# Rows, feature parts, masks and PSUM copies given other engines, with a new order of every queue

## The chip, the cores and the metric

One core of one Trainium2 chip. The time is device microseconds of one execution of the whole program, the median of several runs. The engines are called as the profile calls them: PE (TensorE), ACT (ScalarE), DVE (VectorE), POOL (GpSimd) and SP (SyncE, which here issues DMAs).

## What is computed

Four blocks, one after the other, on a sequence of 2048 tokens of width 512 with 32 heads of 16: attention with a compressive memory (A), a linear attention (B), then A and B once more. Each block adds its result to x.

```
def _A_ref(x, wq, wk, wv, wo, beta):            # x has been layer-normed
    ...
    for s in range(N):                          # N = 4 segments of L = 512 tokens
        qs, ks, vs = (q[:, :, s].copy(), k[:, :, s].copy(), v[:, :, s].copy())
        logits = jnp.einsum('bhqd,bhkd->bhqk', qs, ks) * scale + mask   # causal in the segment
        p = _softmax(logits, axis=-1)
        a_dot = jnp.einsum('bhqk,bhkd->bhqd', p, vs)
        pq = phi(qs)                            # phi(t) = t + 1 where t > 0, else exp(t)
        num = jnp.einsum('bhld,bhde->bhle', pq, M)
        den = jnp.einsum('bhld,bhd->bhl', pq, z)[..., None] + 1e-06
        o = g * (num / den) + (1.0 - g) * a_dot
        outs.append(o)
        pk = phi(ks)
        M = M + jnp.einsum('bhld,bhle->bhde', pk, vs)
        z = z + jnp.einsum('bhld->bhd', pk)
    ...
x = x + _A_ref(_layernorm(x, axis=-1), A_wq, A_wk, A_wv, A_wo, A_beta)
x = x + _B_ref(_layernorm(x, axis=-1), B_wqkv, B_w_phi, B_wo)
```

B projects to q, k and v, makes of q and of k the softmax features of a small product per head (and of its negative), sums feature-times-value over all tokens, and divides as usual.

## The kernel before, in words

**Tiles.** x stays in SBUF as 16 tiles of 128 tokens by 512. A layer (L is 0 or 1) is one A and one B. It is staged by segment s = 0 to 3 of four tiles:

- `ln` makes the layer norm of a segment. For each tile DVE takes the statistics (L786, L787), POOL raises the variance to the power -1/2 (L798) or ACT does it by logarithm and exponential (L792, L793), and DVE makes the normalised rows `xn` (L802, one instruction a tile with two scalars a row). A DMA on SP's queue, or PE with a copy out of PSUM, transposes them.
- `a_proj` projects to keys, queries and values. PSUM is emptied by copies (`k.copy`, `q.copy`, `v.copy`, all at L563) that either ACT or DVE can do. For the memory it makes phi as the smaller of exp(t) and max(t + 1, 1): ACT makes the exponential (L933, L958), DVE the linear part (`phik.lin` L934, `phiq.lin` L959) and the minimum (L935, L960). `lo` (L892) and `kp` (L923) are copies within SBUF.
- `a_att` is the attention inside the segment. Its scores come in units of 2048 columns of PSUM, and each unit is read by two exponentials (L1103) of 128x1024. There are 36 of them in a segment and 288 in the program. Units with a diagonal block are masked after the exponential: two products with the mask `modd` for the odd heads (`mask.odd`, L1109, DVE or POOL) and one `affine_select` in place for the even heads (`mask.even`, L1112, POOL). `mask.even` comes after both `mask.odd` of its tile, since it overwrites what they read. Then PE multiplies with the values, and DVE divides (L1137, L1138).
- `a_out` projects the result and adds it to x. `b_keys`, `b_queries` and `b_out` are the linear attention: `b_keys` adds up over the segments what `b_out` multiplies with, so `b_out` of a layer starts when `b_keys` of segment 3 is complete. The next layer's first `ln` follows `b_out` of segment 0. This passage between the 144th exponential (the last of layer 0) and the 145th (the first of layer 1) is called the boundary here; what comes after the 288th is called the tail.

**The order of the work.** Nothing is scheduled at run time. The functions above only list 3388 operations with their reads and writes. Four tables say the rest. `ORDER` names every operation once; the order of the names, taken for each engine alone, is the order of that engine's queue (a negative entry is a filler of some matmuls into an unused part of PSUM). `ENGINE` has one letter (a, d, p, s) for each operation that several engines can do, in the order in which the functions list them. `SLOTS` says which buffer a tile gets. `AFTER` is a list of pairs (x, y): operation x also waits for operation y, beyond what its data ask for. `replay` (L354) reads them, and `finalize` (L407) writes the instructions and the semaphore waits.

`either` (L559) lists an operation that DVE or POOL can do, with the time of each that was assumed; `dve`, `pool` and `act` list one for a single engine.

Of the kernel before, what the change touches and what calls it, by code (L numbers as in the profile page):

```python
# [8 lines left out]
ALU = mybir.AluOpType  # L9
AX = mybir.AxisListType  # L10
BF16 = mybir.dt.bfloat16
# [512 lines left out]
class Kernel:  # L524
# [65 lines left out]
    def sb(self, name, shape, dt):  # L590
        return self.es.enter_context(self.nc.sbuf_tensor(name, shape, dt))
# [891 lines left out]
```

## Time and profile before

| | |
|---|---|
| three runs | 442.88, 443.93, 445.04 us; median 443.93 us |
| the profiled execution | span 442.2 us from the first instruction to the last; no other time is given for it |
| granted TensorE clock | 0.996 |
| instructions with busy time | PE 7894, DVE 1032, ACT 625, POOL 446 |
| the first exponential of the attention starts | 12.82 us |
| the 144th starts; the 145th starts | 182.84 us; 221.22 us |
| the 288th ends | 397.97 us |

How to read it: an engine's busy time is the time in which at least one of its instructions runs. ACT, DVE and PE overlap the end of one instruction with the start of the next, so that the mean duration of an instruction is more than what it takes of its engine's time; lines that give the time of several equal instructions in a row show the latter. A wait is put down to the engine that ended it.

### The profile page before, as it was taken

The numbers are of one execution on the slowest core, as the hardware profiler recorded it, in microseconds if no ns is written. First come the engines' busy times: TensorE is split into PE (matmuls) and PEld (weight loads), VectorE is DVE, ScalarE is ACT, GpSimd is POOL, SyncE is SP. The second block draws the span as 40 slices with busy tenths as digits, with TensorE's granted clock in tenths as the row PEclk, the third lists the DMA queues.
The fourth block names the chain that finished last, engine by engine and source line by source line (L and its number), as shares of the span: only waits on it lengthen the run. The fifth ranks groups of instructions, "written<-read, shape, count | busy, mean of one in ns | idle before, by whom it ended". The sixth has DMA issues, their size and how long they took to land.

```text
span 442.2 us, 18441 instructions
## 1 busy us (share of the span) xinstructions
PE 423.6 (96%) x7894; PEld 295.4 (67%) x7955; DVE 414.2 (94%) x1032; ACT 406.9 (92%) x625; POOL 268.3 (61%) x446
## 2 busy tenths in 40 slices
PE   7999999999999999999999999999999999999997
PEld 6877767666756665757777666776576665575763
DVE  6999999999999998799999999999899999979997
ACT  3999999999999999997799999999999999999731
POOL 4587679656676687331364778567766767744200
PEclk9999999999999999999999999999899999999999
DMA  8999532517212521532665335444135333032396
GB/s 241 203 221 131 96 51 50 96 29 97 50 26 49 67 35 31 94 61 51 128 75 86 64 73 99 75 72 75 27 39 85 44 57 51 1 74 45 69 164 203
DMA packets 117201, 36.35 MB, mean 82 GB/s; under 512 B 108928, under 2 KB 117120, under 8 KB 117120
## 3 DMA queue, kind: packets, MB, share of 16 engines
q1 hardware_dynamic: 114432, 32.80, 43.2%
q10 hardware_dynamic: 2688, 2.37, 1.7%
q8 instruction: 63, 1.03, 1.0%
q14 instruction: 18, 0.15, 0.1%
HBM read 6.32 MB, written 2.10 MB: 19 GB/s over the span
## 4 chain that ended last, share of the span: by engine, by line
ACT 65%; PE 29%; DVE 4%; issue 1%
ACT PT L1103 49%; PE PS L504 27%; ACT Ek L1199 6%; ACT phi L958 3%; ACT phi L933 2%; ACT K L1282 2%; PE PS L1438 1%; PE PS L585 1%; ACT ktok L563 1%; DVE Vt L1227 1%; ACT VT L563 1%; ACT EQ L1282 1%; ACT QT L563 1%; DVE KV L1254 1%; DVE Rkv L1256 1%
## 5 line engine op out<-in xcount | busy, mean ns | idle before, releaser
L1103 ACT ACTIVATE PT<-PS 128x1024 bf16<-128x1024 f32 x288 | 281.8, 1112 | 1.6 <-PE PS L504 1.1
L1109 POOL TENSOR_TENSOR D<-PT,modd 128x256 bf16<-128x256 bf16 x130 | 85.8, 674 | 43.5 <-ACT PT L1103 13.2
L1112 POOL TENSOR_SCALAR_AFFINE_SELECT PT<-PT 128x512 bf16<-128x512 bf16 x128 | 80.8, 642 | 35.0 <-DVE D L1109 21.6
L504 PEld LDWEIGHTS PS<-VT,PT 128*128 128x128 bf16 x2048 | 74.1, 96 | 15.3 <-ACT PT L1103 1.6
L504 PE MATMUL PS<-VT,PT 128*128 128x17 bf16 x2048 | 79.6, 171 | 0.9 <-ACT PT L1103 0.4
L504 PE MATMUL PS<-VT,D 128*128 128x17 bf16 x512 | 59.7, 171 | 0.1
L504 PE MATMUL PS<-QT,K 32*128 32x64 bf16 (+2 forms) x2176 | 56.0, 213 | 1.6 <-ACT PT L1103 0.8
L786 DVE BATCH_NORM_STATS2 stats<-X 128x6 f32<-128x512 bf16 x64 | 43.0, 681 | 1.7 <-DMA X<-in_A_x_dram 1.4
L504 PEld LDWEIGHTS PS<-VT,D 128*128 128x128 bf16 x512 | 43.2, 96 | 0.2 <-issue 0.2
L1164 DVE TENSOR_TENSOR X<-X,PS 128x512 bf16<-128x512 bf16 x60 | 40.0, 675 | 2.9 <-PE PS L504 2.1
L504 PEld LDWEIGHTS PS<-QT,K 32*128 32x128 bf16 x2176 | 29.5, 93 | 18.7 <-ACT PT L1103 11.5
L1227 DVE TENSOR_TENSOR Vt<-PS,Zk 128x1024 bf16<-128x1024 f32 (+1 forms) x34 | 38.8, 1153 | 1.2 <-PE PS L504 0.9
L1199 ACT ACTIVATE Ek<-PS 128x512 bf16<-128x512 f32 x64 | 38.0, 682 | 1.1 <-PE PS L504 1.0
L1109 DVE TENSOR_TENSOR D<-PT,modd 128x256 bf16<-128x256 bf16 x126 | 35.0, 302 | 1.2 <-PE PS L504 0.7
L504 PE MATMUL PS<-WA_v,xA 128*128 128x256 bf16 x256 | 35.2, 273 | 0.1
L504 PE MATMUL PS<-WA_k,xA 128*128 128x256 bf16 x256 | 34.7, 275 | 0.3 <-ACT PT L1103 0.2
L504 PE MATMUL PS<-xA,WA_q 128*128 128x256 bf16 (+1 forms) x272 | 34.4, 267 | 0.1
L1302 POOL COPY O<-rho 128x512 bf16<-128x512 bf16 x29 | 16.9, 616 | 25.3 <-PE PS L504 9.1
L504 PE MATMUL PS<-WA_o,OT 128*128 128x512 bf16 x113 | 30.5, 380 | 1.7 <-issue 0.5
L1206 POOL TENSOR_TENSOR Vt<-Ek 128x512 f32<-128x512 bf16 x24 | 27.6, 1154 | 6.8 <-ACT Ek L1199 5.3
L1138 DVE TENSOR_TENSOR O<-PS,r 128x256 bf16<-128x256 f32 (+1 forms) x72 | 27.4, 385 | 1.2
L504 PEld LDWEIGHTS PS<-WA_k,xA 128*128 128x128 bf16 x256 | 23.2, 98 | 6.6 <-ACT PT L1103 1.1
(163 smaller groups left out, 921.1 us busy)
## 6 DMA issues: line engine op xcount, KB each, us to landing
X<-in_A_x_dram SPq DMA_DIRECT2D x3, 512.0 KB, 7.5
out_dram<-X ACTq DMA_DIRECT2D x10, 128.0 KB, 2.1
EQ<-in_B_wqkv_dram SPq DMA_DIRECT2D x2, 512.0 KB, 7.1
out_dram<-X SPq DMA_DIRECT2D x6, 128.0 KB, 2.4
OT<-O SPq DMA_TRANSPOSE x36, 3.2
WA_o<-in_A_wo_dram SPq DMA_DIRECT2D x1, 512.0 KB, 6.4
WB_v<-in_B_wqkv_dram SPq DMA_DIRECT2D x1, 512.0 KB, 7.1
WB_o<-in_B_wo_dram SPq DMA_DIRECT2D x1, 512.0 KB, 3.9
```

The costliest lines, as they stand in the source:

```text
L504: return e.matmul(o, l, r, start=st, stop=sp, tile_position=(basep(l), basep(o)))
L786: self.dve(lambda e, t=t, src=src: e.bn_stats(self.stats[:, t, :], src()), 0.603, [held() if held else R("X", t)], [R("stats", t)], name=" ...
L958: self.act(lambda e, t3=t3, src=src, two=two: e.activation(two(), src(), ACT.Exp), 512, [sres], [t3()], name="phiq.exp", cost=0.48)
L1103: self.act(lambda e, st=st, pt=pt: e.activation(pt.ap[:].rearrange("p b c -> p (b c)"), self.ps[:, st.slot[0] * 512:st.slot[0] * 512 + 102 ...
L1109: self.either(lambda e, d=d, k=k, pt=pt: e.tensor_tensor(d.ap[:, :, k, :].rearrange("p b (z c) -> p b z c", z=2), self.ends(pt.ap[:, :, 25 ...
L1112: self.pool(lambda e, q=quarters: e.affine_select(q(), q(), [[0, 4], [1, 128]], ALU.is_ge, 0.0, base=0, channel_multiplier=-1), 0.6, [pt() ...
L1138: self.dve(lambda e, r1=r1, view=view, nt=nt, g=g, o=o[ts]: e.tensor_tensor(o.ap[:, 0:nt, g, :].rearrange("p i (h d) -> p i h d", d=DH), v ...
L1164: self.dve(lambda e: e.tensor_tensor(X[:, t, :], X[:, t, :], self.bank(gen), ALU.add), 0.6, [R("X", t), gen()], [R("X", t)], name="resid")
L1199: self.act(lambda e, sgn=sgn, Ek=Ek, gen=gen: e.activation(Ek.ap[:, sgn, :], self.bank(gen), ACT.Exp, scale=1.0 - 2.0 * sgn), 512, [gen()] ...
L1206: self.pool(lambda e, Ek=Ek, sums=sums: e.tensor_tensor(sums(), *(Ek.ap[:].rearrange("p s (h j) -> p s h j", h=H)[:, :, :, 8 * k:8 * k + 8 ...
L1227: self.dve(lambda e, w=w, n=n, Vt=Vt, Zk=Zk, gen2=gen2: e.tensor_tensor(self.signed(Vt)[:, w, :, 0:16], self.bank(gen2).rearrange("p (h d) ...
L1302: P.add(("act", "pool"), {"act": lambda e, dst=dst, src=src: e.activation(dst(), src(), ACT.Copy), "pool": lambda e, dst=dst, src=src: e.t ...
```

## The change

Four operations get a second engine, and one constant is added for that:

- `xn` (L802) may be done by DVE or POOL.
- `phik.lin` (L934) and `phiq.lin` (L959) may be done by DVE or POOL.
- `mask.even` (L1112) may be done by POOL as before, or by DVE as a product with a triangular mask `tri` of 128x128 that POOL makes once in `setup` by two more instructions.

```
+        self.tri = sb("tri", [128, 128], BF16)
...
+        pool(lambda e: e.memset(self.tri[:], 1.0), 0.2, (), [R("tri")], name="tri")
+        pool(lambda e: e.affine_select(self.tri[:], self.tri[:], [[1, 128]], ALU.is_ge, 0.0, base=0, channel_multiplier=-1), 0.3, [R("tri")], [R("tri")], name="tri")
...
-                self.dve(lambda e, t=t, n=n, xn=xn: e.tensor_scalar(xn.ap[:, n], self.X[:, t, :], self.mv[:, t, 0:1], self.rstd[:, t:t + 1],
+                self.either(lambda e, t=t, n=n, xn=xn: e.tensor_scalar(xn.ap[:, n], self.X[:, t, :], self.mv[:, t, 0:1], self.rstd[:, t:t + 1],
...
-                    self.dve(lambda e, kt=kt, dst=dst: e.tensor_scalar(heads(dst()), self.spread(kt), 1.0, 1.0, op0=ALU.add, op1=ALU.max), 0.21, [kt()], [res], port=True, name="phik.lin")
+                    self.either(lambda e, kt=kt, dst=dst: e.tensor_scalar(heads(dst()), self.spread(kt), 1.0, 1.0, op0=ALU.add, op1=ALU.max), 0.21, 0.62, [kt()], [res], name="phik.lin")
...
-                    self.pool(lambda e, q=quarters: e.affine_select(q(), q(), [[0, 4], [1, 128]], ALU.is_ge, 0.0, base=0, channel_multiplier=-1), 0.6, [pt()], [pt("e")], name="mask.even")
+                    P.add(("dve", "pool"), {"dve": lambda e, q=quarters: e.tensor_tensor(q(), q(), self.tri[:, None, :].to_broadcast([128, 4, 128]), ALU.mult),
+                                            "pool": lambda e, q=quarters: e.affine_select(q(), q(), [[0, 4], [1, 128]], ALU.is_ge, 0.0, base=0, channel_multiplier=-1)},
+                          {"dve": 0.336, "pool": 0.6}, [pt(), R("tri")], [pt("e")], lat=0.05, port=True, name="mask.even")
```

`phiq.lin` changes as `phik.lin` does. All four tables are new. `ORDER` names 3390 operations and 6 fillers with 45 matmuls (before: 14 fillers with 67). `AFTER` has 36 pairs (before: 173). Read along the list of operations, the letters of `ENGINE` give these counts (instructions before -> after):

| operation | ACT | DVE | POOL |
|---|---|---|---|
| `xn` | | 64 -> 5 | 0 -> 59 |
| `phik.lin`, `phiq.lin` | | 46 -> 30 | 0 -> 16 |
| `mask.even` | | 0 -> 2 | 128 -> 126 |
| `mask.odd` | | 126 -> 162 | 130 -> 94 |
| `k.copy`, `q.copy`, `v.copy`, `fold.copy` (PSUM, 512 wide) | 36 -> 24 | 66 -> 78 | |
| `xnT.copy`, `boT.copy` (PSUM, after a transpose by PE) | 16 -> 9 | 4 -> 11 | |
| `kp`, `lo` | 1 -> 0 | 29 -> 20 | 34 -> 44 |
| `bk.z`, `bq.wide` | 5 -> 0 | 6 -> 1 | 53 -> 63 |

The place of an operation in `ORDER` against the four marks (first, 144th, 145th and last exponential in ACT's queue) says in which stretch it is issued. Between the first and the 144th, ACT's queue has 3 `v.copy`, one `k.copy`, one `q.copy` and one `fold.copy` fewer. In the boundary it has 4 `xnT.copy`, one `bq.wide` and one `bk.z` fewer. Between the 145th and the last it has two each of `k.copy`, `q.copy` and `v.copy`, one `lo` and one `bk.z` fewer and one small `bq.ln` more. In the tail it has 3 `boT.copy`, 2 `bq.wide` and one `bq.ln` fewer.

PE's queue has, in the boundary, 2 steps of `bk`, 3 of `bout` (two 512-wide matmuls each), one `bo` (8 matmuls), 2 steps of `kv` (4 each), 2 of `bq.sum` (16 each) and 4 of `pv` (8 each) fewer, which stand in the stretches before and after it. In the tail it has 2 steps of `bk`, 2 of `bq` and 5 of `pv` fewer.

More of the change, by code (lines that the diff above doesn't have):

```diff
@@ L33 @@
 ORDER = (
[134 rows of a table removed]
[135 rows of a table added]
 )
 AFTER = (
[17 rows of a table removed]
[4 rows of a table added]
 )
 ENGINE = (
-    "aaddpaadpaapadapaaddddpapddaddddppdpdpddddpdppppppppdppppddppdpddapaddddpaddddddaddddaddpdpdpppppdppppppddddppddddppddpppdpppdddpdddddpapdda"
-    "ddpdddpdpdddpdppppppdddddddpdpppddddddppppppddppdpppppddddpddadaddddddpdddddpppppppadppdddpdddddppdddddppdppdpddpppdddppddaadpapppppaaaaaada"
-    "papdpadaaadddddapdaaddddddddppdddpdddppdppppppddppddpdpddadadadapaddpdadapppppappppppdppdpdddddpdddpdpdppppppppdpddddapdpadadapdddaapddadppp"
-    "pppppppddddpddddddddddpppdpddpppppddppddpdddpdpdadpdddpddddddpppppppddddppddddddpdpdpddppppdppddddppddppdddappppapppasaassaaasasaaasaaaa"
+    "dadapdpdpaadpadpadapaapddpdpappdddpdpdpppppdppddpddpddpdppdppdpppdppppdppddppdpddpppppddpdddaddapdpdpdpddpdpddddddadddddddpppdppppppppddpppp"
@@ new lines @@
+    "pppddpppppdppdpddpddpdpddpddpddppdddppddpddpddpppppdpdadddpaddddpdpddddpddpdpdppppppppppppddpddpdppddpddppdpddpddpddpppdpppdpppppppddppppddp"
+    "ddpppppdpdpdddpdpdpdpdddpdddddpppppdppppppddppdpddppdpdpdddpdppddpddddpddpddpdppdddpppdpdppddpddpppdpappppppppaaaapdpdpdpdpappddadpaaapddddp"
+    "dddddaddpddppdppppdppddpdppddpddpdppppppppddpdpppdpddppppppdpddpaddadddapdppapddddpapdpppppppppppppppdpppppdppddpdppddppdpddppppppppppdpddpd"
+    "ppddpddppdpppdpapddpaddaddpdpdpddpapddddpdpppppppppppppdpddpddppdpppppdpddpdppddddpdpppdpddpppppppdppdppddppppddddpdpdddddddpdddpdddddpppdpp"
@@ L193 @@
+    "ppppppddpddpdppddpddpddpddppppddddpddppppdppddddpddppppddpddpppdpappppppppaadssaaaaasaaaasdsds"
 )
 SLOTS = (
-    "30101150011223200020110010002313101120134730120130561306072238931260120031343012032004317301151224020321063154592010111207206821031601011502"
-    "16910100178210111016201005100020321400235903114250236703320315013241060013031202612230714134920250001257235606812710630313130200121000001021"
-    "15235702104022304013013003901020001333160010001100021201110148021221131200020116920200010100184200110321201110201202040130961003201510324830"
@@ L198 @@
-    "32570101300012011010100313169130060702024831036213353010450230127012030810322412030313016270134531063082120011122101113701001320112002802145"
-    "10000002120100317302405002341602051089021014003020215012453003410233501141602050001110030203000100057202201420136451271006022110112200270110"
-    "63021145120208902145012023200101210002312136007051100021400102011220261200015102000132220371213017236121100021300203302631071011026111842010"
-    "10400521010012102105100403121200012911341220101062020105910110300021431022010110068012311460503130027901100011233101030001000241002121002030"
@@ L206 @@
-    "10011114120413167126004108912600710021211030511031002003023410200011441060014111532000040012230151202200102134702100201106123200154501303404"
-    "1513609146175129003332003351015622307"
+    "10112020011032140192010001161203150217016013322004150246327164783213007160331201210013015310612332709213617187210060011271106412706312120161"
+    "02117420015821219110212031273131200670461313001731171321270628223405300215603453422305114002113702010010901018212010365100201301243000422502"
+    "01903261175011240752010324362000013401053122011100132450254087031321133102225033364102212131335010211783031345124203101109010013320451351303"
@@ new lines @@
+    "32020236132601725130209321412403005024125115301302273100011367683111230030310032025913161121717132162053212254139300050862041501234135703593"
+    "20041142301504761000673232545002100512109220040503204120041106072038211612003502120271712001216113101214601002332210820101023131104501123101"
+    "20167102032211280132393031453005303220130713100326200104130006612012111772003130700637000221602200407611000200232013233300534050202303861013"
+    "20660402012000331200041562131138611021951221017320121010410011330121210911001085012221021371001320240031000430521130693014501230221012115200"
@@ new lines @@
+    "46022490032158313121401002130020100331126930203010120062022540102820350002430102001501118402014206702100231221951000013120627141202011100231"
+    "31110810211000259102330204523030232120142176305023020023041150013803220495201011103122061726210678732111501410230200402035230067691210602131"
+    "10761453230701312272132316708221013210710312130543110600704051623613393172301610101031212137047121126217520952314070212334362354142011000911"
+    "20115410200630201040291326732243170060121707121212602318217016242231040500570200141617016138127310122101101033120140050693020223022421002001"
@@ L208 @@
+    "30122101792010301436560201418202214424320601410601301203931330053041150072501506102321100300363013114014302211652200320240321012056770116012"
+    "1715096223270103234213032643761801704"
 )
@@ L801, in ln @@
             for n, t in enumerate(4 * c + i for i in grp):
-                self.dve(lambda e, t=t, n=n, xn=xn: e.tensor_scalar(xn.ap[:, n], self.X[:, t, :], self.mv[:, t, 0:1], self.rstd[:, t:t + 1],
-                                                                    op0=ALU.subtract, op1=ALU.mult), 0.324,
-                         [R("X", t), R("mv", t), R("rstd", t)], [xn(n)], port=True, name="xn")
+                self.either(lambda e, t=t, n=n, xn=xn: e.tensor_scalar(xn.ap[:, n], self.X[:, t, :], self.mv[:, t, 0:1], self.rstd[:, t:t + 1],
+                                                                       op0=ALU.subtract, op1=ALU.mult), 0.324, 0.65,
+                            [R("X", t), R("mv", t), R("rstd", t)], [xn(n)], name="xn")
             if len(grp) == 2:
@@ L958, in a_proj @@
                         self.act(lambda e, t3=t3, src=src, two=two: e.activation(two(), src(), ACT.Exp), 512, [sres], [t3()], name="phiq.exp", cost=0.48)
-                        self.dve(lambda e, dst=dst, src=src: e.tensor_scalar(dst(), src(), 1.0, 1.0, op0=ALU.add, op1=ALU.max), 0.21, [sres], [res], port=True, name="phiq.lin")
+                        self.either(lambda e, dst=dst, src=src: e.tensor_scalar(dst(), src(), 1.0, 1.0, op0=ALU.add, op1=ALU.max), 0.21, 0.62, [sres], [res], name="phiq.lin")
                         self.dve(lambda e, two=two, dst=dst: e.tensor_tensor(dst(), dst(), two(), ALU.min), 0.334, [res, t3()], [res], port=True, name="phiq.min")
```

4 lines of the change are left out of this document (removed), and 290 rows, old and new, of tables (AFTER, ORDER).

## The prediction

> **What bounds the kernel now.** I read the page's busy shares and slices first, then the busy times in five stretches cut at the marks of the attention (front, layer 0, boundary, layer 1, tail), then the chain that ended last, as a whole and in the two stretches without exponentials.
>
> ```profile
> span 442.2 us, 18441 instructions
> PE 423.6 (96%) x7894; PEld 295.4 (67%) x7955; DVE 414.2 (94%) x1032; ACT 406.9 (92%) x625; POOL 268.3 (61%) x446
> PE   7999999999999999999999999999999999999997
> DVE  6999999999999998799999999999899999979997
> ACT  3999999999999999997799999999999999999731
> POOL 4587679656676687331364778567766767744200
> ACT 65%; PE 29%; DVE 4%; issue 1%
> ```
>
> ```profile
> 0.00:12.82 12.82, 10.56 (x120) 8.92 (x121) 8.97 (x32) 5.79 (x11) 5.80 (x21) 1.00 0.87 256
> 12.82:183.90 171.08, 164.43 (x3466) 116.78 (x3487) 162.93 (x430) 170.96 (x225) 122.42 (x200) 1.00 0.49 82
> 183.90:221.20 37.30, 36.62 (x419) 25.05 (x421) 36.59 (x78) 29.74 (x81) 10.56 (x18) 1.00 0.37 72
> 221.20:397.97 176.77, 171.50 (x3510) 119.61 (x3536) 166.24 (x427) 175.19 (x232) 122.04 (x195) 0.99 0.40 62
> 397.97:442.20 44.23, 40.44 (x395) 25.02 (x396) 39.47 (x69) 25.25 (x81) 7.52 (x14) 0.99 0.55 120
> ...
> ```
>
> ```profile
> by line: PE PS L504 72.8%; PE PS L585 5.8%; DVE Rkv L1256 3.5%; DVE KV L1254 3.4%; DVE Vt L1227 3.3%; ACT Ek L1199 2.8%; issue 1.7%; PE PS L1438 1.6%; ACT OT L563 1.5%; DVE EQ L1308 1.5%; ACT Vt L1219 0.9%; ACT Zk L1215 0.6%; ACT Zk L1214 0
> by line: PE PS L504 55.8%; issue 4.5%; DVE Vt L1227 4.3%; DVE PT L1338 4.1%; PE PS L585 3.6%; DVE KV L1254 2.9%; DVE Rkv L1256 2.9%; DVE X L1164 2.7%; DVE PhiK L1308 2.6%; DVE Zk L1210 2.2%; DVE EQ L1308 1.3%; ACT xB L563 1.3%; ACT O L1302
> ```
>
> The columns of the second fence are the stretch, its length, then the busy time of PE, PE's weight loads, DVE, ACT and POOL. ACT is busy for 170.96 of 171.08 us in layer 0 and for 175.19 of 176.77 in layer 1: there it sets the pace, and the whole chain is ACT for 65%. PE looks nearly as full, but its digits are weak evidence, as the first row below says: a weight load waited 72 times for an exponential, so PE is held by ACT. DVE has 8.2 us to spare in layer 0 and 10.5 in layer 1. In the boundary (37.3 us) and the tail (44.2 us) ACT is no bound; the last fence, the chains of these two, gives PE 72.8% and 55.8% of them.
>
> ```profile
> PEld PS L504 <- ACT PT L1103: 25.9, 72, 0.8
> 84.35 14.67 ACT PT L1103 x16
> 359.20 1.96 ACT Ek L1199 x4
> 187.37 5.61 PE PS L504 x26
> 176.55 8.42 PE PS L504 x221
> L802 DVE TENSOR_SCALAR xn<-X,mv,rstd 128x512 bf16<-128x512 bf16 x64 | 24.4, 404 | 1.4 <-POOL rstd L798 1.1
> 94.47 0.49 DVE L1109 TENSOR_TENSOR D<-PT,modd 128x256 bf16<-128x256 bf16 x2
> L1109 DVE TENSOR_TENSOR D<-PT,modd 128x256 bf16<-128x256 bf16 x126 | 35.0, 302 | 1.2 <-PE PS L504 0.7
> L563 DVE CAST VT<-PS 128x512 bf16<-128x512 f32 x21 | 14.2, 676 | 0.5 <-PE PS L504 0.4
> L934 DVE TENSOR_SCALAR PhiK<-ktok 128x512 bf16<-128x512 bf16 x22 | 6.4, 293 | 0.0
> L960 DVE TENSOR_TENSOR PhiQ<-PhiQ,phi 128x512 bf16<-128x512 bf16 x24 | 10.1, 424 | 0.1
> L1254 DVE TENSOR_TENSOR KV<-KV,PS 128x408 f32<-128x408 f32 x12 | 6.7, 573 | 1.7 <-PE PS L504 1.7
> L1308 DVE TENSOR_TENSOR EQ<-EQ,OT 128x1024 bf16<-128x1024 bf16 x8 | 5.3, 673 | 0.0
> 89.02 1.29 POOL L1109 TENSOR_TENSOR D<-PT,modd 128x256 bf16<-128x256 bf16 x2
> L1112 POOL TENSOR_SCALAR_AFFINE_SELECT PT<-PT 128x512 bf16<-128x512 bf16 x128 | 80.8, 642 | 35.0 <-DVE D L1109 21.6
> L1302 POOL COPY O<-rho 128x512 bf16<-128x512 bf16 x29 | 16.9, 616 | 25.3 <-PE PS L504 9.1
> L1206 POOL TENSOR_TENSOR Vt<-Ek 128x512 f32<-128x512 bf16 x24 | 27.6, 1154 | 6.8 <-ACT Ek L1199 5.3
> ```
>
> **Prices.** In a queue an exponential takes 14.67/16 = 0.92 us, a 512-wide activation 1.96/4 = 0.49, a 512-wide matmul 5.61/26 = 0.216, a narrow one 8.42/221 = 0.038. Two masks on DVE took 0.49, one lasts 0.302: the second added 0.19, so 0.11 of each DVE instruction lies under the next. With that overlap `xn` costs DVE 0.404 - 0.11 = 0.29, a linear part 0.18, a 512-wide copy out of PSUM 0.676 - 0.11 = 0.57, a sum of 0.573 in `kv.add` 0.46, a product L1308 0.56, and the new even mask, which no row shows on DVE, 0.31 by the nearest product of the same size (L960, 0.424); doubled, its two instructions would cost 0.6 us more in all. A mask on POOL costs 1.29/2 = 0.65. `xn` and the linear parts on POOL are not in this trace. Below stands a 512-wide copy there (0.616), above a 512-wide product with two tensor inputs (1.154). I take 0.65: they read one tensor, as the copy and the `affine_select` (0.642) do. Less than the copy is not to be had, since they read and write as much.
>
> The Trainium skill (GPSIMD Engine Reference, Engine selection) speaks against this edit: elementwise work belongs on VectorE, GpSimd being about half as fast with two inputs, while one input runs at roughly line rate. The copy's 0.616 beside the product's 1.154 agrees with both halves; by the two-input half the 59 rows and 16 linear parts would put 38 us more on POOL than I count.
>
> **Layer 0.** ACT loses six copies (3 `v`, one each of `k`, `q`, `fold`): 6 x 0.49 = 2.9 us, and with almost no idle time there, the stretch shortens by that, to 168.1. It does so only if nothing else is late. DVE: 25 rows go (-7.3), 9 linear parts (-1.6), 3 `kp`, 3 `lo` and 2 `bk.z` (about -1, at a linear part's price or less); 24 odd masks (+4.6), 2 even masks (+0.6), six copies (+3.4), and from the boundary two `kv.add` and two L1308 (+2.0) come. That is +0.7: 163.6 of 168.1. POOL gives up 23 odd masks and an even one (-15.6), takes 34 rows and linear parts (34 x 0.65 = +22.1; at 1.154 +39.2) and nine small copies (+3.5 estimated from about 0.4 each): 132 of 168 (at 1.154: 150). POOL would have to pay 1.7 us a row before it alone fills the stretch. A row on POOL waits for POOL's own L798 and for no new engine; the masks queued behind it come 0.65 us later each time, and with them PE's products with the values, while SP's transposes, the same in number, now wait for POOL. I cost that at nothing, since ten PT tiles let the exponentials run ahead of the masks; if that lead is used up, each row costs its 0.65 us (the second and third rival).
>
> **Layer 1.** ACT loses six copies, 2.9 us, a `lo` and a `bk.z` and gets a small logarithm, together some 0.3 less (estimated; the three are far smaller than a copy): -3.2. The 1.6 us of idle time stay: 173.6. DVE: 24 rows (-7.0), 5 linear parts (-0.9), 13 odd masks (+2.5), six copies (+3.4), some two us of single steps from boundary and tail: unchanged at 166.
>
> **Boundary.** Here the new order does the work: PE's queue loses 10 wide matmuls (2.2 us) and 80 narrow ones (3.0), 5.2 in all, and DVE loses its six rows, two `kv.add` and two L1308 (-3.8). What leaves is then issued in the two layers, where PE waits for ACT and hides it; without that cover it would cost its 5.2 us again. PE is 72.8% of this chain, so 3.8 of the 5.2 us count; the row, now made on POOL, comes 0.25 us later for the tile that is awaited. I take 3.5, with 0 and 5.2 as the ends. **Tail.** PE loses 8 wide and 40 narrow matmuls, 3.2 us; at 55.8% that is 1.8, and two rows on POOL cost some of it: 1.5, ends -0.5 and 3.2. **Front.** The first two rows stay on DVE, the two instructions for `tri` run on POOL while x loads: 0, at worst 0.5 lost.
>
> Sum: 2.9 + 3.2 + 3.5 + 1.5 = 11.1 us. The profiled execution's span of 442.2 becomes 431.1. The median of the runs, 443.93, lies 1.7 above that span; the same on top gives **433 us**. About 0.5% (2.2 us) is what a measurement can tell from no change here.
>
> **The rivals.**
>
> ```profile
> 385.99 0.64 POOL L1112 TENSOR_SCALAR_AFFINE_SELECT PT<-PT 128x512 bf16<-128x512 bf16 x1 [1.44 <-DVE xn L802]
> 76.54 0.63 POOL L1112 TENSOR_SCALAR_AFFINE_SELECT PT<-PT 128x512 bf16<-128x512 bf16 x1
> 76.87 0.58 DVE L960 TENSOR_TENSOR PhiQ<-PhiQ,phi 128x512 bf16<-128x512 bf16 x1
> POOL PT L1112 <- DVE D L1109: 21.6, 26, 3.3
> POOL D L1109 <- DVE D L1109: 7.5, 10, 1.9
> ```
>
> *DVE held up by POOL: slower.* The two engines do not run everything side by side. A product on DVE that began 0.33 us into a mask of POOL took 0.58 instead of 0.424: POOL held something until about 0.49 into its 0.63. In the first row an even mask stood for 1.44 us until `xn` on DVE was done, of which it needs nothing; that is one of the 173 pairs of `AFTER`, which keep POOL from starting where DVE is about to need the same path. Only 36 remain, so more of the waiting may fall to DVE. DVE will issue 304 instructions within SBUF that may be held (162 + 2 masks, 5 rows, 30 linear parts, 46 minima, 20 copies, 23 sums, 16 products; 350 before). POOL, 268 us now and some 300 then (75 rows and linear parts at 0.65 more, 36 odd masks less, some twenty small copies more), holds the path for 0.49/0.63 of it, 233 of 431 us, 54%. Met at random, 304 x 0.54 x 0.25 (half of 0.49) = 41 us of stalls. DVE has 168.1 - 163.6 and 173.6 - 166 to spare, 12 us: stalls beyond 12 us (0.04 an instruction) lengthen the program, beyond 23 they eat the whole gain. At three quarters of random, 31 us, it comes to 433 + 19 = 452 us. For it: POOL's queue gets longer work, and waits fall away. Against it: DVE has 46 such instructions less, and many pairs are covered by data: the 21.6 and 7.5 us that masks waited for DVE's masks will partly be kept by their reads and writes.
>
> The Trainium skill (SBUF — State Buffer, Who interferes with whom) states that VectorE and GpSimd share a pair of ports under an exclusive lock, taken by whoever starts first and held for the whole instruction. The late product agrees, though it was let in before the mask ended; by the rule's whole instruction the stalls at random would be 304 x 0.70 x 0.31 = 66 us and the time near 487, estimated from that page.
>
> *Half of that.* Stalls of about 20 us, or rows at 1.154 on POOL that let transposes and masks come late, leave 439 to 446.
>
> *PE is the bound: no change.* If PE's 164.43 of 171.08 us were real work, taking 2.9 us from ACT would change nothing: 443.9, and the moved matmuls would cost in the layers what they save in the boundary. For it: the digits of 9. Against it: 0.92 us an exponential without a gap, and PE's own waits for them.
>
> *Boundary and tail follow in full.* With 5.2 and 3.2 us there, and the idle 1.6 us of layer 1 gone, it is 433 - 5 = 428.
>
> **How the numbers follow.** Forecast (428 to 439): 0.62. Full gain, below 428: 0.09. Half of it lost, 439 to 446: 0.12, of which 0.07 is faster by over 0.5% (below 441.7) and 0.05 the same. Slower through DVE's stalls: 0.11. PE's bound, no change: 0.06. So faster 0.78, same 0.11, slower 0.11. The range runs from 426 to 444: it leaves out the slower rival and the far end of the full gain.
>
> **What would show it.** `xn` with 59 instructions on POOL of 0.6 to 0.7 us; ACT's busy time near 396 us and still 98% or more in both layers; 168 and 173 us from first to last exponential; a boundary near 34 and a tail near 43. Held DVE would show as a mean above 0.302 in its odd masks and idle time before them put down to POOL, and as ACT's idle time in the layers. The prediction is wrong if ACT falls below 95% there, or if the boundary does not shorten although PE has less in it.

## The result

The changed kernel takes 539.81 us (median of 538.35 to 546.07), the kernel before 444.48 (442.88 to 445.04) on the same chip: a ratio of 1.2172 (95% interval 1.2103 to 1.2241). It is 95.3 us slower, where 11 less were forecast. The profiled execution took 538.35 us, 536.5 of them from the first instruction to the last, at a granted TensorE clock of 0.929 (before 0.996).

The page of the kernel after: busy times, ACT's slices, the granted clock in the same slices, and the chain that ended last, by engine.

```profile
span 536.5 us, 18394 instructions
PE 448.6 (84%) x7872; PEld 302.4 (56%) x7933; DVE 434.2 (81%) x1000; ACT 405.1 (75%) x600; POOL 411.8 (77%) x505
ACT  1876839886988989967548984868877889998740
PEclk8889869987999999999979996989969889999999
POOL 33%; DVE 27%; PE 24%; ACT 6%; DMA 5%; issue 4%; SPq 0%; POOLq 0%; DVEq 0%
```

Most of the digits of 9 are gone from ACT's row, and no engine has taken them over. ACT held 65% of the chain; now POOL has 33%, DVE 27 and PE 24. Such a chain, handed on from engine to engine, is the sign of work that waits for single results and not for one full engine. PE's own 448.6 us beside 423.6 are no extra work, with fewer instructions (7872, before 7894): its granted clock was lower, in the front (0.82) and in the layers (0.93 and 0.91, as the next view shows).

The five stretches (columns as in the prediction), cut at 19.18, 228.1, 273.8 and 489.05 us:

```profile
0.00:19.18 19.18, 12.90 (x128) 10.86 (x129) 9.09 (x31) 5.88 (x11) 10.22 (x27) 0.82 0.90 274
19.18:228.10 208.92, 171.32 (x3425) 117.31 (x3448) 176.64 (x421) 172.78 (x219) 181.29 (x214) 0.93 0.35 58
228.10:273.80 45.70, 37.73 (x428) 25.30 (x434) 34.84 (x68) 27.88 (x74) 26.79 (x28) 0.99 0.37 61
273.80:489.05 215.25, 186.27 (x3492) 123.99 (x3518) 173.57 (x412) 176.20 (x224) 180.79 (x221) 0.91 0.31 51
489.05:536.50 47.45, 40.40 (x409) 24.98 (x410) 40.01 (x69) 22.33 (x75) 12.68 (x18) 0.99 0.52 112
```

The front is 6.4 us longer, layer 0 37.8, the boundary 8.4, layer 1 38.5 and the tail 3.2. In layer 0 ACT is busy for 172.78 of 208.92 us, POOL for 181.29 and DVE for 176.64; each of the three is above the 168.1 us that were forecast for the whole stretch.

The costly groups (idle time before an instruction is the column behind the second bar), and the row of `xn` with shortest, median and longest in ns:

```profile
L1096 ACT ACTIVATE PT<-PS 128x1024 bf16<-128x1024 f32 x288 | 278.0, 1034 | 50.8 <-PE PS L494 49.3
L795 POOL TENSOR_SCALAR xn<-X,mv,rstd 128x512 bf16<-128x512 bf16 x59 | 126.1, 2140 | 12.0 <-ACT rstd L786 6.6
L952 POOL TENSOR_SCALAR PhiQ<-QT 128x512 bf16<-128x512 bf16 x10 | 19.3, 1931 | 0.9 <-DVE D L1102 0.4
L953 DVE TENSOR_TENSOR PhiQ<-PhiQ,phi 128x512 bf16<-128x512 bf16 x24 | 14.1, 586 | 7.2 <-POOL PhiQ L952 7.0 <-ACT phi L951 0.2
L1102 DVE TENSOR_TENSOR D<-PT,modd 128x256 bf16<-128x256 bf16 x162 | 52.7, 348 | 2.6 <-ACT PT L1096 2.0
L795 POOL TENSOR_SCALAR xn<-X,mv,rstd x59: 2070/2086/2702, 14.0 to 496.7; 128x512 bf16<-128x512 bf16 x59
```

ACT stands idle before the exponentials for 49.3 us because of PE. `xn` lasts 2.14 us on POOL and a linear part 1.93, three times what the prediction took. DVE stood 7.0 us before its minima for linear parts on POOL (the fourth line), its minima went from 424 to 586 ns and its odd masks from 302 to 348. Who waits for whom, three of the largest:

```profile
ACT PT L1096 <- PE PS L494: 49.3, 41, 4.5
PE PS L494 <- POOL PT L1106: 24.6, 15, 3.7
POOL PT L1106 <- DVE D L1102: 21.2, 23, 3.4
```

One place in full: the chain that ended last between 178 and 189 us, with start and length of each piece, then the first matmuls behind it and the exponential of their result, with their waits in brackets.

```profile
178.90 0.24 POOL rstd L789
...
179.21 0.73 POOL rstd L791
...
180.04 4.78 POOL xn L795 x2
...
184.84 3.21 DMA xB<-xn
...
188.09 2.55 PE PS L494 x36
```

```profile
188.09 1.04 PE L494 MATMUL PS<-WB_k,xB 128*128 128x512 bf16 x4 [1.77 <-DMA xB<-xn]
189.17 1.08 ACT L1194 ACTIVATE Ek<-PS 128x512 bf16<-128x512 f32 x2 [1.34 <-PE PS L494]
```

Two rows made one behind the other take 4.78 us, their transpose can start only then, PE stands for 1.77 us and ACT after it for 1.34. Before, two rows took DVE 0.81 (twice the 0.404 of one).

The front is another matter. Its chain, and PE in the four microseconds in which its wait ended (busy time of PE, its loads, DVE, ACT, POOL, then the granted clock):

```profile
2.78 9.46 DMA WA_q<-in_A_wq_dram
13.81 3.13 PE PS L494 x32
10.00:14.00 4.00, 1.63 (x16) 1.66 (x17) 2.37 (x11) 0.16 (x1) 1.08 (x2) 0.50 1.12 333
```

The half of `WA_q` on SP's queue is issued 0.6 us later than before (2.78 for 2.18 us). A quarter of X (512 KB), which stood behind it, now stands ahead of it; 768 KB of `WA_o` and `WA_v` follow it at once, which SP's queue did not have in the first 12 us before; and ACT's half of `WA_v` is issued at 3.26 us in place of 8.76. It lands after 9.46 us in place of 6.3. PE stood for 5.0 us, its granted clock was 0.50 from 10 to 14 us, and 32 matmuls that took 1.80 us before took 3.13.

### The profile page after: what moved, and what is told of

Read it like the earlier page. It is cut to its first block, busy times and chain, and to the rows that moved or that the text cites. A ratio compares the mean times of both kernels' runs of the same rounds, so it can differ in the third digit from the quotient of the medians.

```text
span 536.5 us, 18394 instructions
## 1 busy us (share of the span) xinstructions
PE 448.6 (84%) x7872; PEld 302.4 (56%) x7933; DVE 434.2 (81%) x1000; ACT 405.1 (75%) x600; POOL 411.8 (77%) x505
## 4 chain that ended last, share of the span: by engine, by line
POOL 33%; DVE 27%; PE 24%; ACT 6%; DMA 5%; issue 4%; SPq 0%; POOLq 0%; DVEq 0%
PE PS L494 24%; POOL xn L795 16%; POOL PT L1106 4%; ACT PT L1096 4%; POOL D L1102 3%; DVE D L1102 3%; DVE X L1159 3%; POOL PhiQ L952 3%; DVE Vt L1222 3%; DVE stats L779 2%; POOL rstd L791 2%; DMA WA_q<-in_A_wq_dram 2%; DVE O L1133 1%; DMA xB<-xn 1%; POOL Vt L1201 1%
## 5 line engine op out<-in xcount | busy, mean ns | idle before, releaser
L1096 ACT ACTIVATE PT<-PS 128x1024 bf16<-128x1024 f32 x288 | 278.0, 1034 | 50.8 <-PE PS L494 49.3
L795 POOL TENSOR_SCALAR xn<-X,mv,rstd 128x512 bf16<-128x512 bf16 x59 | 126.1, 2140 | 12.0 <-ACT rstd L786 6.6
L1106 POOL TENSOR_SCALAR_AFFINE_SELECT PT<-PT 128x512 bf16<-128x512 bf16 x126 | 80.4, 652 | 27.3 <-DVE D L1102 21.2
L1102 POOL TENSOR_TENSOR D<-PT,modd 128x256 bf16<-128x256 bf16 x94 | 64.9, 700 | 8.1 <-DVE D L1102 2.8
L494 PE MATMUL PS<-QT,K 32*128 32x64 bf16 (+2 forms) x2176 | 59.2, 222 | 3.1 <-DVE O L1133 1.9
L1102 DVE TENSOR_TENSOR D<-PT,modd 128x256 bf16<-128x256 bf16 x162 | 52.7, 348 | 2.6 <-ACT PT L1096 2.0
L494 PE MATMUL PS<-xA,WA_q 128*128 128x256 bf16 (+1 forms) x272 | 38.4, 284 | 7.4 <-DMA WA_q<-in_A_wq_dram 5.0
L494 PE MATMUL PS<-WA_k,xA 128*128 128x256 bf16 x256 | 38.0, 287 | 5.5 <-DVE PhiQ L953 2.9
L494 PE MATMUL PS<-WA_v,xA 128*128 128x256 bf16 x256 | 38.7, 287 | 0.4 <-ACT PT L1096 0.3
L1132 DVE RECIPROCAL r<-PS 128x16 f32<-128x16 f32 (+1 forms) x72 | 16.8, 235 | 22.5 <-PE PS L494 22.3
L494 PEld LDWEIGHTS PS<-xA,WA_q 128*128 128x128 bf16 x272 | 24.9, 104 | 16.8 <-issue 6.7
```

Source lines behind the costliest of these rows:

```text
L494: return e.matmul(o, l, r, start=st, stop=sp, tile_position=(basep(l), basep(o)))
L795: self.either(lambda e, t=t, n=n, xn=xn: e.tensor_scalar(xn.ap[:, n], self.X[:, t, :], self.mv[:, t, 0:1], self.rstd[:, t:t + 1], op0=ALU. ...
L1096: self.act(lambda e, st=st, pt=pt: e.activation(pt.ap[:].rearrange("p b c -> p (b c)"), self.ps[:, st.slot[0] * 512:st.slot[0] * 512 + 102 ...
L1102: self.either(lambda e, d=d, k=k, pt=pt: e.tensor_tensor(d.ap[:, :, k, :].rearrange("p b (z c) -> p b z c", z=2), self.ends(pt.ap[:, :, 25 ...
L1106: "pool": lambda e, q=quarters: e.affine_select(q(), q(), [[0, 4], [1, 128]], ALU.is_ge, 0.0, base=0, channel_multiplier=-1)},
L1132: self.dve(lambda e, r1=r1, view=view, nt=nt: e.reciprocal(r1.ap[:, 0:nt, :], view()[:, :, :, 16]), 0.07 + 0.0475 * nt, [pv()], [r1()], na ...
```

## The experiments

Four theories were open. *Price*: a row and a linear part cost POOL three times 0.65 us, and this alone fills it and delays what stands behind it. *Held*: DVE is held up by POOL, since `AFTER` has 137 pairs fewer. *Loads*: the new order of the DMAs in the front. *Fit*: the new order is an order for assumed times and engines; where these are off, waits arise whose sum no engine's load shows. Ratios are to the kernel before on the same chip.

**The price by itself.** A kernel of its own: POOL makes six instructions of a kind, one behind the other, while DVE rests; then rows, copies and products with 16 small products of DVE (128x256) beside them.

> Not the reference's work: it copies x to the output and runs GpSimd instructions by themselves, six of each kind, 128x512 bf16 unless said: tensor_scalar with two operations and two scalars a row (as the normalised rows), with one operation and a scalar a row, with two operations and immediate scalars (as the linear parts), with one immediate, copy, product of two tensors, then rows of 256 and 1024 columns; VectorE is idle. After that rows, copies and products again while VectorE makes masks. Price theory (the two-operation tensor_scalar is slow on GpSimd in itself): rows 2.0 to 2.1 us and linear parts 1.9 with VectorE idle, copy 0.6, product 1.15, and one operation clearly below two. Contention theory (it costs 0.65 as the copy does, and VectorE's use of a shared path stretched it to 2.1): 0.6 to 0.7 with VectorE idle, about 2 only beside the masks.

POOL's timeline: start, length of six, what.

```profile
4.43 12.34 POOL L27 TENSOR_SCALAR o<-x,s 128x512 bf16<-128x512 bf16 x6 [2.69 <-DMA x<-in_A_x_dram]
16.87 9.26 POOL L30 TENSOR_SCALAR o<-x,s 128x512 bf16<-128x512 bf16 x6
26.22 11.35 POOL L33 TENSOR_SCALAR o<-x 128x512 bf16<-128x512 bf16 x6
37.66 8.76 POOL L36 TENSOR_SCALAR o<-x 128x512 bf16<-128x512 bf16 x6
46.48 3.39 POOL L38 COPY o<-x 128x512 bf16<-128x512 bf16 x6
49.95 6.68 POOL L39 TENSOR_TENSOR o<-x,y 128x512 bf16<-128x512 bf16 x6
...
90.87 3.83 POOL L27 TENSOR_SCALAR o<-x,s 128x512 bf16<-128x512 bf16 x1
```

So without DVE a row costs 12.34/6 = 2.06 us, the linear part's form (two operations with constants) 1.89, one operation 1.46 with a constant and 1.54 with a scalar a row, a copy 0.565, a product of two tensors 1.11. Rows of 256 and 1024 columns took 1.22 and 3.78 in the mean:

```profile
L27 POOL TENSOR_SCALAR o<-x,s 128x1024 bf16<-128x1024 bf16 x6 | 22.6, 3779 | 0.1
L27 POOL TENSOR_SCALAR o<-x,s 128x256 bf16<-128x256 bf16 x6 | 7.2, 1218 | 0.1
```

That is some 3.3 ns for each column more. It is `tensor_scalar` on POOL that is dear; the number of tensors that it reads does not tell its price. The Trainium skill (GPSIMD Engine Reference, Engine selection) has one-input work run at roughly line rate and two-input work about twice as slow as on VectorE. The product fits roughly: its 1.11 us are 2.6 times the 0.424 of DVE's product of this size (L960 before). This instruction, with one tensor input, is nearly twice as dear as the product, so for it the measurement decides and not the rule. The last line of POOL's timeline is a single row with DVE's products beside it: it took 3.83 us, so the two engines do slow one another, and POOL can be the one that pays.

**Rows on POOL in the order before.** One line of the kernel before, all 64 rows.

```
-                self.dve(lambda e, t=t, n=n, xn=xn: e.tensor_scalar(xn.ap[:, n], ...
+                self.pool(lambda e, t=t, n=n, xn=xn: e.tensor_scalar(xn.ap[:, n], ...
```

> The kernel before with its own order, and one edit: all 64 normalised rows on GpSimd. Price theory: GpSimd gets 64 x 2.1 = 134 us on its 268, some 400 us, and the masks behind each row come 2 us late: 490 to 560 us. Order theory and contention theory at 0.65 a row (42 us more on GpSimd): 440 to 460 us.

548.6 us, 1.2351 (1.2303 to 1.24). This one edit costs 104 us. And the same with `e.tensor_copy(xn.ap[:, n], self.X[:, t, :])` in place of the row:

> The kernel before with all 64 normalised rows on GpSimd, as in the run with 549 us, but each as a copy of 0.57 us (rows not normalised). Price theory: the 104 us that the rows cost go but for some waits: 445 to 465 us. If it were the place of the rows in GpSimd's queue, behind masks, and not their length: above 500 us.

451.91 us, 1.0166 (1.0137 to 1.0194). The groups of the two kernels and the largest wait of the first:

```profile
L802 POOL TENSOR_SCALAR xn<-X,mv,rstd 128x512 bf16<-128x512 bf16 x64 | 135.7, 2126 | 10.7 <-ACT rstd L793 7.3
PE PS L504 <- POOL PT L1112: 41.0, 21, 6.2
```

```profile
L802 POOL COPY xn<-X 128x512 bf16<-128x512 bf16 x64 | 39.7, 642 | 13.0 <-ACT rstd L793 9.4
```

Same place, same waits, same queues: a row of 2.126 us or of 0.642. The difference, 96.7 us over 64 rows, is 1.51 us each, in the mean as much as the 1.48 that a row costs more, although POOL is busy for only 82% of layer 0 (177.52 of 215.5 us): the masks queued behind the row come late, and with them the products with the values, which is the second line (41.0 us). The 1.51 us are not shown row by row, and they hold more than the row: PE is busy for 460.9 us at a granted clock of 0.916, with copies for 425.0 at 0.992. DVE held by the long rows can be only a little of it, since its busy time is 412.1 us with them and 406.3 with copies. At the price that the prediction took, moving the rows costs 7.4 us in this order, 0.12 us a row: little, but not nothing.

**Cheap rows in the changed kernel.** POOL's rows and linear parts are copies; nothing else differs from the kernel after.

```
-                self.either(lambda e, ...: e.tensor_scalar(xn.ap[:, n], self.X[:, t, :], self.mv[...], self.rstd[...], ...
+                self.P.add(("dve", "pool"), {"dve": ..., "pool": lambda e, ...: e.tensor_copy(xn.ap[:, n], self.X[:, t, :])},
```

> The changed kernel, with every normalised row and linear part that it has on GpSimd replaced by a copy of the same shape (0.57 us by itself), so the rows there aren't normalised and the linear parts there are copies; order, buffers and waits stay. Price theory (the order is sound, and the 2 us of an instruction that it counts at 0.65 cost everything): 430 to 445 us. Order theory (it is bad even with the times that it counts on): 490 us or more.

465.54 us, 1.0479 (1.0428 to 1.053): 74.3 of the 95.3 us hang on the price. Its stretches from layer 0 on, the row, and ACT's waits:

```profile
18.80:195.60 176.80, 163.49 (x3427) 114.97 (x3452) 167.26 (x422) 170.42 (x219) 131.97 (x214) 0.99 0.42 69
195.60:233.30 37.70, 36.46 (x428) 24.92 (x431) 35.11 (x71) 27.78 (x75) 16.66 (x30) 1.00 0.46 69
233.30:416.40 183.10, 172.34 (x3498) 119.01 (x3523) 167.41 (x411) 173.74 (x225) 135.03 (x218) 0.99 0.39 61
416.40:461.50 45.10, 40.09 (x404) 24.90 (x405) 39.46 (x69) 22.16 (x76) 9.73 (x18) 1.00 0.55 118
L797 POOL COPY xn<-X 128x512 bf16<-128x512 bf16 x59 | 37.1, 642 | 13.5 <-ACT rstd L786 6.8
ACT PT L1099 <- PE PS L494: 12.3, 22, 2.9
```

With copies POOL is at 131.97 us in layer 0, the prediction's 132 to the digit, and ACT waits for PE 12.3 us instead of 49.3. Yet it is 21 us slower than before: no stretch is shorter, neither the layers (176.8 and 183.1; 168.1 and 173.6 forecast) nor the boundary (37.7; 34) nor the tail (45.1; 43).

**Rows back on DVE.** The kernel after, in `replay`:

```
+            if op.name in ("xn", "phik.lin", "phiq.lin"):
+                op.on = "dve"
```

> The changed kernel with its order, masks and copies, but all normalised rows and linear parts back on VectorE. Price theory: 75 instructions of 2 us leave GpSimd, its busy time falls from 412 to about 262 us, and the time comes to 430 to 455 us. Order theory (the new order of the queues and the 137 pairs of AFTER that are gone cost the time): it stays above 500 us, with ScalarE idle in the attention as before.

513.64 us, 1.1543 (1.1492 to 1.1594). Without any dear instruction on POOL it is still 69 us slower than before. The price is therefore not a sum that is added to an order: the order has the rows where POOL has time, and DVE comes to them when it comes to them. A part of the 69 us can also be DVE's load, 444.8 us busy where it had 414.2. POOL's masks stood for DVE's 57.8 us where the changed kernel has 21.2:

```profile
POOL PT L1108 <- DVE D L1104: 57.8, 43, 6.9
```

The next run goes further: the new order with the letters of the kernel before for all but the PSUM copies and stores.

> The changed kernel's order, buffers and AFTER with the engines of the kernel before for everything but the PSUM copies (rows, linear parts, masks, small copies), so that each engine has the work of before, ScalarE less. Load theory for the 514 us of the run with the rows back on VectorE (there VectorE had rows and the 36 extra masks, 20 us too much): 440 to 460 us. Fit theory (an order made for other engines and times makes the queues wait, whatever the load): above 480 us.

537.83 us, 1.2082 (1.2007 to 1.2158). As slow as the changed kernel, with not one of the rows on POOL: the new order can cost as much by itself. Whether by its fit alone, this run doesn't show. DVE is busy for 455.6 us, 41.4 more than before, of which 19 copies at the prediction's 0.57 make 10.8; the rest is in longer instructions, as its odd masks show (302 ns before):

```profile
L1102 DVE TENSOR_TENSOR D<-PT,modd 128x256 bf16<-128x256 bf16 x126 | 44.0, 365 | 6.4 <-PE PS L494 5.2 <-ACT PT L1096 1.0
```

So waits at the wrong places and a DVE held by POOL's other work stand side by side here.

**The loads.** The kernel with cheap rows, and in `ORDER` one quarter of X on SP's queue put behind `wphi`, and ACT's half of `WA_v` put later.

```
-    ... 65, 76, 11, 6, 66, 4, 69, 7, 8, -401, 60, 61, ... 77, 87, 12, 38, ... 92, 325, 9, ...
+    ... 65, 76, 6, 66, 4, 69, 7, -401, 60, 61, ... 77, 87, 12, 11, 38, ... 92, 325, 8, 9, ...
```

> As the run before it, and besides the first loads in nearly the order of the kernel before: the load of the second quarter of x on SyncE's queue after that of the second half of WA_q and the small one, and ScalarE's half of WA_v later. In the changed kernel the first exponential starts at 19.2 us instead of 12.8, behind a WA_q that took 9.5 us to land. If the loads' order is the cause: 5 to 6 us less than the run before it, with the first exponential at 13 to 14 us. If it isn't: within 1 us of it.

461.54 us (459.4 to 463.42), 1.0387 (1.0335 to 1.0438); the first exponential at 16.5 us in place of 18.8. Some 4 us by the medians, 2.3 in the front itself.

**The pairs.** The kernel before without the loop `for x, y in AFTER: ops[x].need.add(y)`:

> The kernel before with none of the 173 extra pairs of AFTER (none of them is needed by the data). Price theory: 440 to 450 us, since the pairs move waits between GpSimd and VectorE by less than the exponentials' lead. Order theory, and the slower rival of the prediction (GpSimd holds up VectorE where it is not kept back): above 455 us, with VectorE's masks longer than 0.302 us in the mean.

453.83 us, 1.0217 (1.019 to 1.0244): the 173 waits were worth 9.6 us. DVE's odd masks, without them:

```profile
L1107 DVE TENSOR_TENSOR D<-PT,modd 128x256 bf16<-128x256 bf16 x126 | 39.1, 334 | 0.6 <-PE PS L502 0.4
```

302 became 334 ns: DVE is held, as the rival had it. The opposite, in the kernel with cheap rows and mended loads: each full-width POOL instruction waits for the last DVE instruction within SBUF that stands before it in `ORDER`.

> The run with cheap rows and the earlier loads (461.5 us; rows and linear parts on GpSimd are copies), and every GpSimd instruction of full width also waits for the last VectorE instruction within SBUF that stands before it in ORDER, so that GpSimd never gets ahead of VectorE where the plan has it behind. Held theory (what is left of the loss, 17 us, is VectorE held by GpSimd since only 36 pairs of AFTER remain; taking all 173 away from the kernel before cost 9 us): 445 to 453 us, and VectorE's odd masks back from 0.321 us to 0.305 or less. Order theory (the new order is longer in itself): 458 us or more.

542.5 us, 1.2169 (1.2107 to 1.2231), with odd masks at 342 ns (321 without these waits). Waits put everywhere cost 81 us and did not shorten what they were to protect. The run doesn't decide how much holding cost in the changed kernel.

**POOL without reads.** The same kernel with cheap rows and mended loads; POOL's masks, rows and linear parts are memsets, so that POOL reads nothing for them (those of the even masks write a quarter of what the mask did). As a control, the kernel before with POOL's masks as memsets.

> The new order with earlier loads (461.5 us), where GpSimd's odd and even masks, rows and linear parts are memsets: they read nothing and are shorter (masks aren't applied, rows aren't normalised). GpSimd then holds back neither VectorE nor the products. Held theory (what remains of the loss is GpSimd's hold on VectorE and its lateness): below 440 us, and 5 us or more under the same edit in the order of before, since ScalarE has 11 us less to do. Order theory (the new order's queues wait in themselves): 450 us or more.

> The kernel before, where GpSimd's odd and even masks are memsets that read nothing (masks aren't applied there); rows stay on VectorE. Control for the run before it. ScalarE's 99% in the layers says that it gains little: 438 to 444 us. If GpSimd's masks were a hidden bound of the kernel before: below 435 us.

455.7 us (453.03 to 455.71 in three runs, 461.38 in a fourth), 1.0295 (1.0227 to 1.0364), and for the control 444.01, 0.999 (0.9976 to 1.0004). Odd masks on DVE and two waits of the first:

```profile
L1112 DVE TENSOR_TENSOR D<-PT,modd 128x256 bf16<-128x256 bf16 x162 | 43.7, 293 | 1.7 <-ACT PT L1106 1.5
POOL PT L1117 <- DVE D L1112: 60.5, 43, 6.0
ACT PT L1106 <- PE PS L501: 8.8, 18, 2.7
```

POOL now idles for 60.5 us before its even masks and DVE's masks are at 293 ns, near the control's; 5.8 us were due to POOL's reads and length. What is left over the kernel before, 11.2 us by the medians and 13 by the ratio, is neither price nor what POOL reads for masks and rows. 2.8 us of it still stand in the front, where the first exponential starts at 15.6 us (12.82 before). In the control DVE's masks fall to 281 ns, and the time doesn't move: being held by POOL's masks cost the kernel before nothing.

**The copies by themselves.** The loads per stretch said that ACT gains 2.9 us a layer where six copies out of PSUM leave it. In the kernel before, only that: 19 copies that the change takes from ACT (`v` 5, `k` 3, `q` 3, `fold` 1, `xnT` 4, `boT` 3) get a d in `ENGINE`.

> The kernel before with only the PSUM copies moved as the change moves them, 19 of them from ScalarE to VectorE. Load theory, as the prediction counted: 2.9 us in each layer, where VectorE has 8 and 10 us to spare: 437 to 441 us. Fit theory (in an order made for other engines each moved copy makes a queue wait, though the loads allow it): 447 us or more.

456.85 us, 1.0274 (1.0249 to 1.0299): slower by 12.2. Layer 0 and the boundary, and ACT's wait for PE (before, it came to 1.1 us):

```profile
12.80:188.90 176.10, 164.86 (x3463) 117.54 (x3484) 166.53 (x436) 169.25 (x219) 121.78 (x200) 0.99 0.45 81
188.90:228.90 40.00, 37.48 (x419) 24.73 (x423) 38.25 (x81) 28.28 (x77) 10.38 (x17) 1.00 0.36 67
ACT PT L1103 <- PE PS L504: 7.2, 12, 1.1
```

ACT did lose its time (169.25 us busy, 170.96 before), DVE has 9.6 us to spare, and the stretch is 5.0 us longer. A copy is awaited: PE needs its bank of PSUM, the next product needs its result. On ACT it stood behind one exponential; in DVE's queue it stands behind what the order put there. The same with POOL's masks as memsets, so that DVE isn't held by them:

> The kernel before with the 19 PSUM copies on VectorE (456.9 us) and GpSimd's masks as memsets. Held theory for the 12 us that the copies cost (VectorE, now fuller, meets GpSimd's masks at other times than the pairs of AFTER provide for): it falls under the control run by 2 us or more. Fit theory (the copies stand late in VectorE's queue, and PE waits for them): 8 us or more above the control.

455.62 us, 1.0248 (1.0221 to 1.0275), 11.6 above its control: so it is not the holding by POOL's masks. Their place in the queue is what is left; which copies are awaited was not shown one by one. One more that the loads would call a gain: `lo`, `bk.z` and `bq.wide`, six small copies, from ACT to POOL in the kernel before, whose POOL is at 61%.

> The kernel before with only the six small copies that ScalarE had (one lo, two bk.z, three bq.wide) on GpSimd; their GpSimd price is in the trace (0.42 to 0.62 us each). Load theory (ScalarE sets the pace in the layers, GpSimd has room): three of the six lie in the layers, so 1 to 1.5 us less: 443 to 444 us. Fit theory (queues made for other times): 445 to 448 us.

445.48 us, 1.0021 (1.0005 to 1.0037). No version of these beats the kernel before; the control at 0.999 leaves work out.

## Why the prediction was wrong

**The step that failed first** is the price: "I take 0.65: they read one tensor, as the copy and the `affine_select` (0.642) do." A row measured 2.09 us (median) and a linear part 1.93; alone, 2.06 and 1.89. The bracket of 0.616 to 1.154 was drawn by the number of tensors read, and both ends were other instructions. The prediction had the point from which it decides, "POOL would have to pay 1.7 us a row before it alone fills the stretch", and the price lies beyond it: by its own arithmetic, with the measured prices, POOL's layer 0 is 122.4 - 15.6 + 25 x 2.09 + 9 x 1.93 + 3.5 = 179.9 us, measured 181.29. Filling POOL is only the smaller part of the loss: the stretch is 40.8 us above the forecast 168.1, and of these 13.2 are POOL's work beyond 168.1 and 27.6 are time in which POOL stood. It should have been carried as the slower rival. Only 1.154 stood as the upper end, though nothing in the trace excluded more.

**Second, the cover.** "I cost that at nothing, since ten PT tiles let the exponentials run ahead of the masks." At 0.642 us the rows on POOL cost the kernel before 7.4 us, 0.12 us a row, so that most of such a row was covered; beyond that the program lost 1.51 us for each 1.48, so that nothing more was. The lead was there, but no longer than the price that was assumed; ACT's busy share does not show how long it is.

**Third, the sum by loads.** "ACT loses six copies [...] the stretch shortens by that": the copies alone made layer 0 5.0 us longer and the program 12.2. The condition "only if nothing else is late" was written down and then checked by busy times alone, which can't show it. So the four terms (2.9, 3.2, 3.5 and 1.5) failed also where price did not enter: with cheap rows no stretch came out shorter. PE's moved matmuls left the boundary at 37.7. In the changed kernel both signs of being wrong that the prediction named came: ACT at 83% and 82% of the layers (172.78 of 208.92 us and 176.20 of 215.25), and a boundary of 45.7 us with less in it.

**The front** was costed at 0, at worst 0.5; it lost 6.4 us, and its chain is a load of weights that landed late. Two loads moved back brought 2.3 us. They are not all of it: with the same loads, the first exponential starts at 16.5 us with cheap rows, at 15.6 without POOL's reads and at 13.7 with pairs everywhere. What makes up the rest was not tested. The loads at the start were no term of the sum.

**The rival of held DVE** was right in its mechanism and not in its weight. DVE's layers hold 176.64 and 173.57 us where the sum gave 163.6 and 166: 20.6 us more, where the rival took 31 and a random meeting 41. The sign that the prediction named came only in half: longer masks, but no idle time before them put down to POOL. ACT's idle time, its other sign, came too, and has other causes besides. Beside layers of 208.92 and 215.25 us this DVE isn't full, so it was one of several that are late. The run without POOL's reads gives 5.8 us at the price of copies; beside the 74.3 us, DVE's same 1000 instructions are busy for 434.2 us with the long rows and linear parts and for 418.2 with copies. How much of these 16.0 us reaches the end was not separated. A single meeting, in the kernel of prices (a row of POOL, then a product of DVE):

```profile
88.82 2.07 POOL L27 TENSOR_SCALAR o<-x,s 128x512 bf16<-128x512 bf16 x1
88.94 0.78 DVE L81 TENSOR_TENSOR p<-x,y 128x256 bf16<-128x256 bf16 x1 [88.94 <-POOL o L27]
```

The product started 0.12 us into a row of 2.07 and took 0.78, where the shortest of its kind took 0.28: it was let in some 0.6 us into the row. The Trainium skill (SBUF — State Buffer, Who interferes with whom) has the lock held for the whole instruction; that section says so of DVE in its two-port modes, and of a product with two inputs in SBUF that it contends with POOL's reads. In this one meeting the measurement says a third of the row. The 487 us that the prediction estimated from the Trainium skill was the nearest to the result of the times on record, by luck for the most part: the runs bear out its reason only in part.

**PE as the bound, and the full gain** are out: PE waits in all stretches.

**The account of the 95.3 us**, by medians: 74.3 price of the rows and linear parts with what follows from it, 4.0 the loads, 5.8 what POOL reads and how long it takes at the price of copies, 11.2 what is left: the order with its letters, and 2.8 us of the front. The runs of these kernels lie up to 8 us apart, so the three small terms are sizes, not digits. The 74.3 hold what a lower clock costs: PE is busy for 448.6 us in the changed kernel and 424.3 with cheap rows (granted clock 0.929 and 0.985); that share was not separated. The four terms hold for edits made in this sequence: putting the rows back on DVE shows that price and order don't simply add. Open: which places make up the last 11.2 (ACT waits for PE 8.8 us in 18 places there), and whether an order made for the true price would gain anything; no such order was made.

## What to carry to other kernels

Take the price of an instruction that is moved to another engine from that instruction on that engine, or leave its upper end open and put the point from which it decides among the rivals; other instructions that read as many tensors are no bracket. In an order written for fixed engines and times, free time of an engine is not the price of what is put there: ask what stands behind the instruction in its new queue and who awaits that. A waiting list such as `AFTER` is part of the tuning, worth 9.6 us (8.4 to 10.8) in the kernel before.

## What the runs showed of the hardware

`tensor_scalar` on POOL costs about 3.3 ns for each column more: 1.22, 2.06 and 3.78 us at 256, 512 and 1024 columns (bf16, 128 partitions, two scalars a row), and 1.46 us at 512 for one operation with a constant; DVE did the same row in 0.40. A row with DVE's products running beside it took 3.83 us in place of 2.07. Around and after PE's wait of 5.0 us in the front the granted clock was lower: 0.50 in the four microseconds from 10 us on and 0.76 in the next five, where 32 matmuls took 3.13 us in place of 1.80 at 1.00 in the kernel before.
